# Softmax-normalisation transfers on GpSimd's queue, more staging for w_in, and multiplications of zeros in planned gaps

## The chip, the cores and the metric

The kernel runs on one core of a Trainium2 chip. TensorE (PE) multiplies matrices into PSUM, ScalarE (ACT) computes activations, VectorE (DVE) does elementwise work, SyncE (SP) and GpSimd (POOL) can start DMA transfers, and 16 DMA engines move the bytes. The metric is the device time of one execution in microseconds (us). Before the change the median of 3 runs was 631.99 us (631.64 to 633.69).

## The reference

Attention with a tanh cap on the scores, then a two-layer feed-forward part:

```
scores = cap * tanh(q @ k.T / sqrt(64) / cap)          # 4 batches, 12 heads, 448 tokens, head size 64
attn   = exp(scores - max);  attn /= sum(attn) + 1e-9
x      = (attn @ v), heads side by side                # 1792 x 768
h      = x @ w_in                                      # 768 x 2048
g      = h * sigmoid(1.702 * h)
out    = g @ w_out                                     # 2048 x 768
```

w_in and w_out reach the device as 64-bit floating-point words, which the kernel decodes itself into pairs of float16 (a high and a low part).

## The kernel before

The work is cut into 24 units, one per batch and pair of heads. A unit computes the transposed scores in four groups of key columns: matmuls into the PSUM tile s, tanh on ACT (t<-s), exp on ACT (p<-t), and then, on PE, the sums of the exponentials (tile sm) and the unnormalised output (tile pa). Units 0 to 7 multiply in float32; from unit 8 on everything is split into float16 pairs, which takes more work on ACT and DVE. When a batch's six units are done, its x feeds the first layer (tile m, weights wi_h and wi_l) and then the second (tile m, weights in wo).

The normalisation of a unit (function attend, lines 674 to 707) takes a small detour, because the reciprocal is cheap only if the 896 sums of a unit lie across many partitions: s4 (tile f) is evicted from sm, then a DMA writes it to the DRAM tile sd, a DMA reads it back as 112 partitions x 8 (rsum), DVE takes the reciprocal (rr), a DMA writes it to the DRAM tile rd, and two DMAs read that back, repeated over the partitions (rb). DVE multiplies rb by the unit's output, and ACT or DVE splits the product into xh and xl. Two units of batch 0 (4 and 5) do without this detour (normalise_direct). For units 0 to 7 the output is first evicted from pa to pu, of which there are two buffers; pa is a single PSUM bank. So pa of unit n+1 can begin once unit n is in pu, and that needs the product of unit n-2.

w_in is loaded in 15 pieces of 64-bit words into a staging area in the later storage of w_out (early_w, three pieces of 1024 words per partition) and decoded by five steps per piece: a shift and two bit operations on DVE, a scaling on ACT or DVE, and the split into wi_h and wi_l.

The order of the work is made by a planner (class Plan). It lists all operations with their dependences, gives each a cost (the tables at lines 34 to 44), lets a forward pass choose for each engine what starts first, a backward pass compute due times, and repeats this 20 times (PASSES). The best order is then emitted, and each engine and each DMA queue runs its instructions strictly in that order. All transfers of the kernel before stand in one queue, SP's (function dma, line 199). The planner chooses between ACT and DVE for the operations that both can do (function scaled).

Of the code around the change: fetch_w (line 491) requests a piece, decode_w (line 510) decodes it, h_unit (line 709) makes one 128-column block of the first layer and writes g, and 16 small matmuls of zeros at the very start (lines 393 and 394) run before the first data arrive.

## Time and profile before

| | |
|---|---|
| median of 3 runs | 631.99 us |
| the profiled execution | 636.09 us, of which 633.9 us from the first to the last instruction |
| busy: PE, DVE, ACT | 618.0, 386.3, 393.0 us |
| mean granted share of PE's clock | 0.993 |
| HBM read and written | 54.93 and 5.66 MB |
| transfers in SP's queue | 36,288 packets, 60.61 MB |

In the profile, an instruction is named by its line, its engine, and the tiles it writes and reads, out<-in, with buffer numbers left out. Line 196 holds all planned matmuls, line 202 all planned DMA issues, lines 153, 161, 177 and 184 the ACT and DVE operations, so the tile names tell what an instruction does. A matmul in float32 makes two records per instruction. "wo" as the source of matmuls or of decoding is the area in which q, k, v and w_in are staged early on. SPq is SP's instruction queue. PE's busy time counts a matmul that runs at half clock as busy.

### The profile page before, as it was taken

How to read it: one execution, taken by the hardware profiler on the slowest of the kernel's cores; microseconds unless marked ns; L12 is line 12 of the kernel's file. 1: busy time of each engine (PE TensorE's matmuls, PEld its weight loads, DVE VectorE, ACT ScalarE, POOL GpSimd, SP SyncE). 2: the span in 40 equal slices, each digit the busy share in tenths (PEclk: the TensorE clock that was granted, in tenths of full speed). 3: DMA queues.
4: the chain of work that ended last, by engine and by line, in shares of the span. 5: the costliest groups of instructions: out<-in, count | busy, mean ns of one | idle time of the engine just before them, and what ended most of it. 6: DMA issues, size and time to landing. Idle time of an engine off the chain costs nothing.

```text
span 633.9 us, 9374 instructions
## 1 busy us (share of the span) xinstructions
PE 618.0 (97%) x3666; PEld 292.3 (46%) x3666; DVE 386.3 (61%) x684; ACT 393.0 (62%) x536; POOL 0.2 (0%) x4
## 2 busy tenths in 40 slices
PE   7987999999999999999999999999999999999995
PEld 3322344454444445445445545445445555555552
DVE  5687988999789866696773466696754113331000
ACT  6997897699798777787666467778647113331000
POOL 0000000000000000000000000000000000000000
PEclk9997999999999999999999999999999999999999
DMA  8968651442466732202322312200111100000000
GB/s 303 412 202 206 224 183 49 149 147 82 130 187 197 226 98 64 77 14 76 91 68 80 95 49 82 76 16 19 22 41 45 30 30 1 1 0 17 29 15 34
DMA packets 36339, 61.28 MB, mean 97 GB/s; under 512 B 13928, under 2 KB 21952, under 8 KB 36288
## 3 DMA queue, kind: packets, MB, share of 16 engines
q1 hardware_dynamic: 36288, 60.61, 30.8%
q8 instruction: 30, 0.49, 0.3%
q14 instruction: 21, 0.17, 0.1%
HBM read 54.93 MB, written 5.66 MB: 96 GB/s over the span
## 4 chain that ended last, share of the span: by engine, by line
PE 93%; DMA 4%; DVE 1%; SPq 1%; ACT 0%; issue 0%; DVEq 0%
PE m L196 70%; PE s L196 10%; PE pa L196 10%; PE sm L196 4%; DMA wo<-in_moe_w_in_dram 1%; DMA sd<-f 1%; DMA rb<-rd 1%; DMA wo<-in_v_dram 1%; DMA wo<-in_q_dram 1%; SPq L202 0%; DVE wi_l L161 0%; DVE wo L161 0%; ACT wi_h L177 0%; DVE rb L161 0%; DVE wo L184 0%
## 5 line engine op out<-in xcount | busy, mean ns | idle before, releaser
L196 PE MATMUL m<-gh,wo 128*128 128x448 f16 x768 | 216.2, 353 | 0.0
L196 PEld LDWEIGHTS <-wo 128*128 128x128 f16 x1152 | 110.8, 98 | 107.9 <-issue 7.0
L196 PE MATMUL m<-xh,wi_h 128*128 128x448 f16 x384 | 135.6, 353 | 0.0
L196 PE MATMUL m<-xl,wi_h 128*128 128x448 f16 x384 | 135.3, 352 | 0.0
L196 PE MATMUL m<-gl,wo 128*128 128x448 f16 x384 | 135.3, 352 | 0.0
L196 PE MATMUL m<-xh,wi_l 128*128 128x448 f16 x384 | 135.3, 352 | 0.0
L153 ACT ACTIVATE t<-s,tsc 128x896 f32<-128x896 f32 x96 | 87.1, 908 | 49.1 <-PE s L196 48.9
L196 PEld LDWEIGHTS <-wi_h 128*128 128x128 f16 x768 | 72.8, 98 | 78.7 <-issue 13.7
L161 DVE SCALAR_TENSOR_TENSOR f<-f,m 128x448 f32<-128x448 f32 x64 | 39.5, 618 | 53.1 <-ACT f L153 52.9
L153 ACT ACTIVATE f<-m 128x448 f32<-128x448 f32 x64 | 34.6, 541 | 58.9 <-PE m L196 57.8
L177 ACT ACTIVATE f<-m 128x448 f32<-128x448 f32 x23 | 12.4, 539 | 83.9 <-PE m L196 75.8
L161 DVE TENSOR_TENSOR ta<-ta,t 128x896 f32<-128x896 f32 (+1 forms) x48 | 41.0, 855 | 32.1 <-ACT t L153 30.8
L153 ACT ACTIVATE t<-t,lnb,capt 128x896 f32<-128x896 f32 (+1 forms) x52 | 52.9, 1018 | 1.4
L161 DVE SCALAR_TENSOR_TENSOR wo<-wo 128x1024 int32<-128x1024 int32 (+3 forms) x50 | 51.8, 1051 | 3.2 <-ACT wo L177 2.6
L196 PEld LDWEIGHTS <-wi_l 128*128 128x128 f16 x384 | 37.6, 98 | 35.1
L161 DVE SCALAR_TENSOR_TENSOR gl<-f,gh 128x448 f16<-128x448 f32 x64 | 39.5, 622 | 16.9 <-ACT gh L177 16.3
L161 DVE TENSOR_TENSOR p<-t,p 128x896 f16<-128x896 f32 (+1 forms) x52 | 48.9, 942 | 1.2 <-ACT p L177 0.9
L196 PE MATMUL s<-qh,kk 128*128 128x448 f16 (+3 forms) x160 | 47.5, 401 | 0.0
L177 ACT ACTIVATE p<-t 128x896 f16<-128x896 f32 (+1 forms) x52 | 43.4, 835 | 1.5
L196 PE MATMUL s<-ql,kk 128*128 128x448 f16 (+1 forms) x128 | 39.5, 352 | 0.0
L177 ACT ACTIVATE gh<-f 128x448 f16<-128x448 f32 x51 | 29.1, 571 | 13.8 <-DVE f L161 13.8
L196 PE MATMUL pa<-p,vh 128*64 128x448 f16 x256 | 35.4, 357 | 0.0
(92 smaller groups left out, 539.0 us busy)
## 6 DMA issues: line engine op xcount, KB each, us to landing
wo<-in_moe_w_in_dram SPq DMA_DIRECT2D x24, 512.0 KB
stg<-in_kx_dram SPq DMA_DIRECT2D x16, 448.0 KB
stg<-in_qx_dram SPq DMA_DIRECT2D x16, 448.0 KB
stg<-in_moe_w_out_dram SPq DMA_DIRECT2D x16, 384.0 KB
wo<-in_moe_w_out_dram SPq DMA_DIRECT2D x16, 384.0 KB
out_dram<-f SPq DMA_DIRECT2D x24, 224.0 KB
rb<-rd SPq DMA_DIRECT2D x44, 112.0 KB
vd<-in_v_dram SPq DMA_DIRECT2D x18, 256.0 KB
```

Of the source, the lines that this page charges most:

```text
L153: self.nc.scalar.activation(real(out), real(in_), func, scale=real(scale), **b)
L161: getattr(self.nc.vector, name)(out=real(out), **{k: real(x) for k, x in ins.items()}, **kw, **a)
L177: self.nc.scalar.activation(real(out), real(in_), AF.Copy, scale=1.0 if f is None else f, **b)
L196: self.nc.tensor.matmul(real(o), real(w), real(x), start=a, stop=z)
```

## The change

Four things are changed together.

1. The five small transfers of attend (sd, rsum, rd and the two of rb) go to GpSimd's queue. The planner gets that queue as an engine of its own, with 1.0 us for an issue and a lag of 3.0 us, where SP's has 0.5 and 2.6.
2. The first four pieces of w_in (the first 512 columns) are staged in the storage of g, which is now one tile; it has room for three pieces. The three places of early_w go to the pieces behind them. All four are requested when the first is decoded (G_AHEAD). Writes of g in batch 0 come after the decoding of these pieces.
3. Where the planner's times leave PE idle by more than 0.5 us before the first use of tile m, matmuls of a 128 x 128 tile of zeros are emitted (keep_busy), one for each 0.06 us.
4. The planner's order changes everywhere as a consequence.

```diff
+G_PIECES = 4
+G_AHEAD = 4
+IDLE_MIN, IDLE_STEP = 0.5, 0.06
-LAG = {"PE": 0.23, "ACT": 0.0, "DVE": 0.0, "SP": 2.6}
-DMA_ISSUE, DMA_BW = 0.5, 0.36
+LAG = {"PE": 0.23, "ACT": 0.0, "DVE": 0.0, "SP": 2.6, "POOL": 3.0}
+DMA_ISSUE, DMA_BW = {"SP": 0.5, "POOL": 1.0}, 0.36
+QUEUES = ("SP", "POOL")
+SMALL = "POOL"
...
-    def dma(self, pairs, mb):
+    def dma(self, pairs, mb, queue="SP"):
+        issuer = {"SP": self.nc.sync, "POOL": self.nc.gpsimd}[queue]
         def emit():
             for o, i in pairs:
-                self.nc.sync.dma_start(real(o), real(i))
-        self.op({"SP": (DMA_ISSUE * len(pairs), emit)}, [p[0] for p in pairs], [p[1] for p in pairs], mb=mb)
+                issuer.dma_start(real(o), real(i))
+        self.op({queue: (DMA_ISSUE[queue] * len(pairs), emit)}, [p[0] for p in pairs], [p[1] for p in pairs], mb=mb)
...
     def emit(self):
         with self.tc.manual_schedule():
+            end = None
             for o in self.order:
+                if o.eng == "PE":
+                    if self.idle_bank is not None:
+                        if any(b.ring is self.idle_bank for b in o.bufs):
+                            self.idle_bank = None
+                        elif end is not None:
+                            self.keep_busy(o.turn, o.start - end)
+                    end = o.end
                 o.emit()
+
+    def keep_busy(self, turn, gap):
+
+        rows, cols = (128, 128) if turn == "full" else (int(x) for x in turn.split("x"))
+        z, out = self.zeros, self.idle_bank["tiles"][0]
+        for _ in range(int((gap - IDLE_MIN) / IDLE_STEP)):
+            self.nc.tensor.matmul(out[:cols, :128], z[:rows, :cols], z[:rows], start=True, stop=True)
...
+    plan.zeros, plan.idle_bank = wz, ps_m
...
-    gt = [sb.tile([P, NFC, S], F16, name=nm) for nm in ("gh", "gl")]
-    gs = [tuple(plan.fixed(t[:, fc]) for t in gt) for fc in range(NFC)]
+    g_s = sb.tile([P, 2 * NFC * S], F16, name="g")
+    gs = [tuple(plan.fixed(g_s[:, (i * NFC + fc) * S:(i * NFC + fc + 1) * S]) for i in range(2)) for fc in range(NFC)]
+
+    early_g = plan.ring([words(g_s[:, i * NW:(i + 1) * NW]) for i in range(2 * NFC * S // NW)])
...
-                st = plan.turn(early_w)
-                early_bufs["w"].append(st.buf)
+                at = "g" if z < G_PIECES else "w"
+                st = plan.turn({"g": early_g, "w": early_w}[at])
+                early_bufs[at].append(st.buf)
...
-        for y in range(z, z + W_AHEAD[m + (c > 0 and m)]):
+        for y in range(z, z + (G_AHEAD if z + 1 < G_PIECES else W_AHEAD[m + (c > 0 and m)])):
...
-        plan.dma([(sd, s4[::32])], 0.02)
+        plan.dma([(sd, s4[::32])], 0.02, SMALL)
...
-        plan.dma([(rs, sd.rearrange("(j g) (p m) -> (g p) j m", g=2, m=RW))], 0.02)
+        plan.dma([(rs, sd.rearrange("(j g) (p m) -> (g p) j m", g=2, m=RW))], 0.02, SMALL)
...
-        plan.dma([(rd.rearrange("j (p m) -> p j m", m=RW), rr)], 0.02)
+        plan.dma([(rd.rearrange("j (p m) -> p j m", m=RW), rr)], 0.02, SMALL)
...
-        plan.dma([(rb[j * D:(j + 1) * D], rd[j:j + 1].to_broadcast([D, S])) for j in range(2)], 0.3)
+        plan.dma([(rb[j * D:(j + 1) * D], rd[j:j + 1].to_broadcast([D, S])) for j in range(2)], 0.3, SMALL)
...
+        plan.after = early_bufs["g"] if b == 0 else []
         plan.scaled(gh, t, GS)
         plan.stt(gl, t, GS, gh, ALU.mult, ALU.subtract, accum_out=fcol())
+        plan.after = []
```

How the order changes is shown at three places. The first is SP's queue while units 1 and 2 are computed. Names carry buffer numbers here; wo_119 is the staging area, and sd, rsum belong to the normalisations of units 0 and 1. Before:

```order
L202 DMA wo_119<-in_moe_w_in_dram 128x1024 x4
L202 DMA sd0_151<-f0_139 4x224
L202 DMA wo_119<-in_v_dram 128x512
L202 DMA wo_119<-in_k_dram 128x448
L202 DMA wo_119<-in_q_dram 128x448
L202 DMA wo_119<-in_moe_w_in_dram 128x1024 x2
L202 DMA sd1_152<-f1_140 4x224
L202 DMA wo_119<-in_v_dram 128x512
L202 DMA wo_119<-in_k_dram 128x448
L202 DMA wo_119<-in_q_dram 128x448
L202 DMA rsum_115<-sd0_151 112x2x4
L202 DMA wo_119<-in_moe_w_in_dram 128x1024 x2
```

Now SP's queue at the same stage:

```order
L209 DMA wo_119<-in_q_dram 128x448
L209 DMA wo_119<-in_moe_w_in_dram 128x1024 x4
L209 DMA wo_119<-in_v_dram 128x512 x2
L209 DMA wo_119<-in_k_dram 128x448
L209 DMA wo_119<-in_q_dram 128x448
L209 DMA kk0_125<-in_k_dram 128x448
L209 DMA qh0_127<-in_q_dram 128x448
L209 DMA kk1_126<-in_k_dram 128x448
L209 DMA g_171<-in_moe_w_in_dram 128x1024 x2
L209 DMA qh1_128<-in_q_dram 128x448
```

No small transfer stands in it. They are in GpSimd's queue, here from its first transfer on:

```order
L209 DMA sd0_151<-f0_139 4x224
L209 DMA rsum_115<-sd0_151 112x2x4
L209 DMA rd0_153<-rr0_149 112x2x4
L209 DMA sd1_152<-f1_140 4x224
L209 DMA rb0_142<-rd0_153 64x448 x2
L209 DMA rsum_115<-sd1_152 112x2x4
L209 DMA sd0_151<-f2_141 4x224
L209 DMA rd1_154<-rr1_150 112x2x4
L209 DMA rsum_115<-sd0_151 112x2x4
L209 DMA rb1_143<-rd1_154 64x448 x2
```

So they no longer stand between the loads of w_in, q, k and v, but in one line among themselves: the transfer rd of unit 0, which needs rr, stands in front of sd of unit 1.

The second place is DVE's queue around the first reciprocal of a normalisation (rr0), which reads rsum of unit 0. Before, 36 planned DVE instructions stood ahead of it, 27 of them decoding w_in, six on w_out and three evictions:

```order
L161 SCALAR_TENSOR_TENSOR wo_119<-wo_119 128x1024
L161 TENSOR_SCALAR wo_119<-wo_119 128x1024
L161 SCALAR_TENSOR_TENSOR wo_119<-wo_119 128x1024
L161 RECIPROCAL rr0_149<-rsum_115 112x8
L161 SCALAR_TENSOR_TENSOR wi_l_118<-wo_119,wi_h_117 128x2x512
L184 TENSOR_SCALAR wo_119<-wo_119 128x1024
```

Now:

```order
L167 SCALAR_TENSOR_TENSOR wo_119<-wo_119 128x1024
L190 TENSOR_SCALAR wi_h_117<-wo_119 128x2x512
L167 RECIPROCAL rr0_149<-rsum_115 112x8
L190 TENSOR_SCALAR wo_119<-wo_119 128x1024
L167 TENSOR_SCALAR wo_119<-wo_119 128x1024
L186 TENSOR_SCALAR f1_140<-sm0_157 128x224
```

There are 22 ahead of it now, all of them decoding w_in. The product of unit 0 (rb0<-pu0,rb0) stood ten rows behind this reciprocal and now stands 13 rows behind it.

The third place is PE's queue where unit 3's output begins (pa0<-p2); before it stood behind the scores and a part of the sums of unit 4:

```order
L196 MATMUL s0_155<-wo_119 128x448 x2
L196 MATMUL sm0_157<-p1_135,ones32_2_75 64x448 x2
L196 MATMUL s1_156<-wo_119 64x448 x2
L196 MATMUL s0_155<-wo_119 128x448 x2
L196 MATMUL pa0_158<-p2_136,wo_119 64x448 x2
L196 MATMUL pa0_158<-p3_137,wo_119 64x448 x2
L196 MATMUL pa0_158<-p4_138,wo_119 64x448 x2
L196 MATMUL pa0_158<-p0_134,wo_119 64x448 x2
```

Now:

```order
L349 LDWEIGHTS wz_89
L349 MATMUL m0_91<-wz_89 32x128
L202 MATMUL sm0_157<-p2_136,ones32_2_75 32x224 x4
L202 MATMUL sm0_157<-p3_137,ones32_2_75 32x224 x4
L202 MATMUL pa0_158<-p2_136,wo_119 64x448 x2
L202 MATMUL pa0_158<-p3_137,wo_119 64x448 x2
L202 MATMUL s0_155<-wo_119 128x448 x2
L202 MATMUL s1_156<-wo_119 128x448 x2
```

Unit 3's output now follows the sums of its own exponentials at once. L349 is the last of three matmuls of zeros at this place, of 14 in all; two stand behind the second row of scores of unit 0, and nine before the first scores of unit 2. The first layer's first matmuls stand behind 57 rows of attention matmuls now, before behind 59. Over the whole program PE changes between kinds of matmul 223 times, with those of zeros, before 210 times.

## Rows read from the trace of the kernel before

**Rows 1.** The busy time of each engine in five stretches of the span (us), with the granted share of PE's clock, the share of the 16 DMA engines and GB/s as the last three columns.

```profile
7.00:20.00 13.00, 13.00 (x77) 3.71 (x74) 10.40 (x18) 12.00 (x13) 0.00 (x0) 1.00 1.03 388
20.00:37.20 17.20, 17.20 (x128) 5.55 (x126) 10.74 (x16) 16.17 (x21) 0.00 (x0) 1.00 0.88 349
37.20:59.90 22.70, 16.47 (x87) 4.89 (x87) 19.06 (x23) 20.01 (x24) 0.00 (x0) 0.85 0.82 205
60.00:100.00 40.00, 40.00 (x217) 14.34 (x215) 36.20 (x46) 34.41 (x45) 0.00 (x0) 1.00 0.52 177
...
220.00:630.00 410.00, 407.54 (x2355) 204.22 (x2353) 202.37 (x353) 210.33 (x288) 0.00 (x0) 1.00 0.16 47
```

**Rows 2.** What PE waited for over the whole span: total us, times, longest.

```profile
PE s L196 <- ACT t L153: 3.8, 4, 1.5
PE pa L196 <- ACT pu L177: 2.4, 1, 2.4
```

**Rows 3.** PE's instructions in groups by form, first of the stretch from 0 to 37.2 us, then (from the line with x64) of the stretch from 0 to 59.8 us; the number behind the x counts the records.

```profile
L196 PE MATMUL s<-wo 64*128 64x448 f32 x48 | 14.1, 684 | 1.4 <-DMA wo<-in_q_dram 1.4
L196 PE MATMUL pa<-p,wo 128*64 128x448 f32 x48 | 11.2, 567 | 0.0
L196 PE MATMUL sm<-p,ones 128*32 128x224 f32 x96 | 5.8, 359 | 0.0
L196 PE MATMUL s<-wo 64*64 64x448 f32 x14 | 3.5, 565 | 0.0
...
L196 PE MATMUL s<-wo 64*128 64x448 f32 x64 | 18.1, 660 | 4.1 <-ACT t L153 2.7 <-DMA wo<-in_q_dram 1.4
L196 PE MATMUL pa<-p,wo 128*64 128x448 f32 x64 | 17.3, 662 | 2.4 <-ACT pu L177 2.4
L196 PE MATMUL sm<-p,ones 128*32 128x224 f32 x128 | 7.9, 359 | 0.0
L196 PE MATMUL s<-wo 64*64 64x448 f32 x20 | 4.8, 562 | 1.0 <-ACT t L153 1.0
L196 PE MATMUL sm<-p,ones 128*64 128x448 f32 x8 | 1.9, 552 | 0.0
```

**Rows 4.** From the chain of work that ended last, in order of time (start, us, what, xcount of records), the pieces that give PE's pace, and its first matmuls; the last two lines lie behind 100 us.

```profile
5.17 4.85 PE s L196 x12
12.93 0.90 PE pa L196 x4
13.83 0.95 PE s L196 x4
16.64 0.94 PE sm L196 x16
100.32 16.00 PE m L196 x84
118.11 1.24 PE m L196 x6
```

**Rows 5.** From the instructions in order of time (start, us, engine, line, operation, tiles), the normalisation of unit 0 from the eviction of its sums to the product, and what followed: the eviction of unit 2's output to pu, and unit 3's output.

```profile
17.60 0.39 DVE L180 TENSOR_SCALAR f<-sm 128x224 f32<-128x224 f32 x1 [1.18 <-PE sm L196]
...
22.68 0.64 SPq L202 DMA_DIRECT2D sd<-f  x1
...
31.96 0.42 SPq L202 DMA_DIRECT2D rsum<-sd  x1
...
40.83 0.20 DVE L161 RECIPROCAL rr<-rsum 112x8 f32<-112x8 f32 x1
...
41.05 0.33 SPq L202 DMA_DIRECT2D rd<-rr  x1
...
45.54 1.15 SPq L202 DMA_DIRECT2D rb<-rd  x2
...
51.07 0.63 DVE L161 TENSOR_TENSOR rb<-pu,rb 128x448 f32<-128x448 f32 x1 [1.16 <-DMA rb<-rd]
...
51.73 0.54 ACT L177 ACTIVATE pu<-pa 128x448 f32<-128x448 f32 x1 [1.33 <-DVE rb L161]
...
52.33 6.13 PE L196 MATMUL pa<-p,wo 128*64 128x448 f32 x16 [2.43 <-ACT pu L177]
```

**Rows 6.** The normalisation of the last unit, from the eviction of its sums to the product, when the DMA engines had little else to do.

```profile
495.57 0.36 ACT L177 ACTIVATE f<-sm 128x224 f32<-128x224 f32 x1 [2.73 <-PE sm L196]
...
503.19 2.45 SPq L202 DMA_DIRECT2D rb<-rd  x2
507.97 0.62 DVE L161 TENSOR_TENSOR rb<-pa,rb 128x448 f32<-128x448 f32 x1 [8.35 <-DMA rb<-rd]
```

**Rows 7.** Groups of ACT's and DVE's instructions between 7 and 60 us by form: what one decoding step takes (busy us, mean ns).

```profile
L177 ACT ACTIVATE wi_h<-wo 128x1024 f16<-128x1024 f32 x5 | 5.9, 1171 | 0.4 <-DVE wo L161 0.4
L177 ACT ACTIVATE wo<-wo 128x1024 f32<-128x1024 f32 x4 | 4.6, 1156 | 0.1
L177 ACT ACTIVATE stg<-stg 128x384 f32<-128x384 f32 x2 | 1.1, 544 | 0.0
...
L161 DVE SCALAR_TENSOR_TENSOR wo<-wo 128x1024 int32<-128x1024 int32 x13 | 15.8, 1226 | 1.9 <-ACT wo L177 1.8
L161 DVE TENSOR_SCALAR wo<-wo 128x1024 int32<-128x1024 int32 x7 | 4.8, 691 | 1.5 <-DMA wo<-in_moe_w_in_dram 1.5
```

**Rows 8.** The 16 matmuls of zeros at the start.

```profile
1.91 1.86 PE L394 MATMUL m<-wz,ones 128*32 128x128 f16 x16 [1.91 <-DVE thr L840]
```

More of the change, by code (lines that the diff above doesn't have):

```diff
@@ L222, in forward @@
         self.start_over()
-        free = {"PE": 0.0, "ACT": ACT_FROM, "DVE": ACT_FROM, "SP": 0.0}
+        free = {"PE": 0.0, "ACT": ACT_FROM, "DVE": ACT_FROM, "SP": 0.0, "POOL": 0.0}
         cand = {e: [o for o in self.ops if e in o.ways and not o.left] for e in free}
-        turn, pipe = None, 0.0
+        turn, pipe = None, dict.fromkeys(QUEUES, 0.0)
         order = []
@@ L255, in forward @@
                 done += LAG["PE"]
-            elif e == "SP":
-                pipe = max(pipe, t + us) + o.mb / DMA_BW
-                done = pipe + LAG[e]
+            elif e in QUEUES:
+                pipe[e] = max(pipe[e], t + us) + o.mb / DMA_BW
+                done = pipe[e] + LAG[e]
             order.append(o)
@@ L261, in forward @@
                 u.left -= 1
-                u.ready = max(u.ready, t + us if u.eng == e and e != "SP" else done + HANDOFF)
+                u.ready = max(u.ready, t + us if u.eng == e and e not in QUEUES else done + HANDOFF)
                 if not u.left:
@@ L274, in backward @@
     def backward(self, order):
-        after = {o: [(u, 0.0 if u.eng == o.eng != "SP" else LAG[o.eng] + HANDOFF) for u in o.users] for o in order}
+        after = {o: [(u, 0.0 if u.eng == o.eng and o.eng not in QUEUES else LAG[o.eng] + HANDOFF) for u in o.users] for o in order}
         turns = {}
@@ L295, in backward @@
         due = {o: end for o in order}
-        free = dict.fromkeys(("PE", "ACT", "DVE", "SP"), end)
+        free = dict.fromkeys(("PE", "ACT", "DVE", *QUEUES), end)
         cand = [o for o in order if not left[o]]
@@ L325, in emit @@
         with self.tc.manual_schedule():
+            end = None
             for o in self.order:
-                o.emit()
+                if o.eng == "PE":
+                    if self.idle_bank is not None:
+                        if any(b.ring is self.idle_bank for b in o.bufs):
+                            self.idle_bank = None
+                        elif end is not None:
+                            self.keep_busy(o.turn, o.start - end)
+                    end = o.end
+                o.emit()
+    def keep_busy(self, turn, gap):
[3 more added lines that the diff above has]
+            self.nc.tensor.matmul(out[:cols, :128], z[:rows, :cols], z[:rows], start=True, stop=True)
 def tile_kernel(tc, q, k, qx, kx, v, cap, w_in, w_out, out):
@@ L453, in fast_path @@
     early_v = plan.ring([t.bitcast(F32).rearrange("p (c d) -> p c d", d=D) for t in room(HALF + 6 * NA, NV, 4)])
-    early_bufs = {"w": [], "a": [], "h": []}
+    early_bufs = {"w": [], "a": [], "h": [], "g": []}
     stg_t = [sb.tile([P, 2 * S], F32, name=f"stg{i}") for i in range(4)]
```

## The prediction

> **What bounds the kernel now.** I read the stretches first. PE is busy without a break at full clock from 60 us to the end of its work: 40.00 of 40.00 us, then 407.54 of the 410 us behind 220, and the missing 2.5 are the tail [rows 1]. A PE that is full there can't be helped by better transfers, so a gain must come from the first 60 us. ACT and DVE don't bound the rest either (202 and 210 of 410 us behind 220), though between 60 and 100 us they are busy for 34.4 and 36.2 of 40 us.
>
> Busy time hides gaps inside matmuls, so I count what PE needed. At its pace of 0.95 us for four records of scores, 0.90 for four of pa, 0.94 for sixteen of sm, and 16.00 / 84 = 0.19 for one of the first layer [rows 4], the 60 + 48 + 96 records up to 37.2 us (two of the 62 scores records belong behind it) are 14.25 + 10.8 + 5.64 = 30.7 us [rows 3]. PE began at 5.17 [rows 4], so it had 32.0 and lost 1.3, at the start where nothing is ready. From there to 59.9 us come 24 records of scores, 16 of pa, 32 of sm, 8 of the wide sm [rows 3] and the first three of the first layer: 5.7 + 3.6 + 1.9 + 1.8 + 0.6 = 13.6 us, and PE had 22.7. It lost 9.1 us there. This is the ceiling for the whole change.
>
> The waits say where [rows 2]: 3.8 us for tanh on ACT (t), 2.4 us for pu. With 16.47 us busy of 22.70 [rows 1], 6.2 us are idle. The sixteen pa records behind the pu wait took 6.13 us [rows 5] where the pace gives 3.6: the granted clock fell to its lower level (1.2 of 2.4 GHz) after these idle times; the stretch shows 0.85 on average [rows 1]. That is 2.5 us more; 0.4 stay unnamed.
>
> Both waits have a history. ACT is busy for 16.2 of 17.2 us before 37.2 us and for 20.0 of 22.7 behind it [rows 1], since it decodes w_in beside tanh and exp. And pu waited for unit 0's normalisation, which took from 17.99 to 51.07 us, 33.1 us [rows 5]: sd was issued 4.7 us after the sums were there, because SP stood at loads of w_in that had no place yet; rsum 9.3 later, rr 8.9 after that.
>
> **The change part by part.** *Transfers on GpSimd's queue.* The waits behind SP's loads go (order, first place). The new deadline: unit 3's output now needs pu after 16 rows of scores, 12 of pa, 7 groups of sm and 14 matmuls of zeros: 15.2 + 10.8 + 6.6 + 0.8 = 33.4 us of PE work, so at 5.17 + 1.3 + 33.4 = 39.9 us. Before it come the eviction (0.54) and the product (0.63) [rows 5], so rb must land by 38.7. Unit 0's sums are complete after 6, 3 and 2 such groups, 5.7 + 2.7 + 1.9 = 10.3 us of PE, and evicted in 0.39: at 17.2. The detour may take 21.5 us. No row shows a transfer from GpSimd. The nearest below is the last unit's detour on SP with idle DMA engines, from 495.93 to 507.97 = 12.0 us [rows 6]; the nearest above is unit 0's, 33.1. What load does to a transfer with no queue ahead: rb took 5.5 us from its issue to the product that waited for it at 45.54 [rows 5], against 4.8 at 503.19 [rows 6], so about 0.7 more. Four such steps give 12.0 + 2.8 = 14.8; for GpSimd's own part and for its queue I add 3 and take 18, nearer to the lower row, because queue order made most of the 33. Then pu is in time and the 2.4 + 2.5 us of pu wait and clock go.
>
> *The staging of w_in.* Six places instead of three let DVE decode early: it was busy for only 10.40 + 10.74 of the 30.2 us before 37.2 [rows 1]. This takes work from ACT: up to the last exponential of unit 4, ACT decoded in four steps on wo, five on wi_h and two on stg, now three, two and one of half size. That is 4 x 1.16 + 1.1 - 0.6 = 5.1 us less [rows 7], against three more evictions (0.36 + 2 x 0.54, [rows 5, 6]) 1.4 us: ACT is there 3.7 us earlier. PE's waits for tanh (3.8) shrink; I take half, 1.9 us, as left, because ACT is still only a step or so ahead of PE. The earlier w_in loads push k, q and v back by up to three pieces of 0.52 MB, 4 us at 388 GB/s [rows 1]; k and q of unit 1 are used only some 8 us after unit 0's begin, so I cost this at nothing; without that cover it would be PE idling 1 to 2 us near 13.
>
> *Zeros.* 14 matmuls of 128 columns are 0.054 us each at the first layer's pace (0.19 x 128 / 448), at most 0.116 by the start's 1.86 us for 16 [rows 8]. Two lie in the start's wait; the other twelve cost 0.7 us (1.4 at most) if PE is not idle there, and nothing if it is. They can't give back more than the clock's 2.5 us, which are counted above.
>
> *Changes between kinds of matmul.* 13 more in the program; one costs 1.24 - 6 x 0.19 = 0.1 us [rows 4], so 1.3 us, or nothing where PE waits.
>
> Sum: 9.1 - 1.9 - 0.7 - 1.3 = 5.2 us gained. The profiled execution took 636.09 us, 4.1 more than the median; the part before 60 us is the same in kind, so I subtract from both: 630.9 and 631.99 - 5.2 = 626.8 us.
>
> A rule that speaks against it: rows 7 show DVE's TENSOR_SCALAR steps at 0.69 us for 1024 words, where the two-input steps take 1.23; nine of the fast ones stand in the new order from eight rows ahead of rr0 to the product. The Trainium skill ("SBUF — State Buffer", section "SBUF: two separate sides") says that a transfer started from GpSimd can't write its descriptors while DVE runs in such a two-port mode, and gives 620 ns alone against about 3100 ns beside a copy. If each of five transfers waits for one whole step of 0.69 us, the detour is 18 + 3.5 = 21.5 us, exactly the deadline, and the sum stands without margin. With the page's figure, an estimate of 5 x 2.5 = 12.4 us more, it would be 30 us and the gain gone. No row here shows either.
>
> **The rivals.** *A: ACT and DVE pay it back.* If PE is 5.2 us ahead at 60 us, DVE's 36.2 us of work up to 100 us [rows 1] must fit into 34.8; unless the early decoding takes it forward, DVE is 1.4 us late, and if ACT's 3.8 us of waits stay whole, 1.9 us more are lost: 5.2 - 3.3 = 1.9, so 630.1. For it: both engines are near 90% there. Against: DVE's idle 9 us before 37.2.
>
> *B: the detour is in time only in part.* Between 21.5 and 26.7 us the gain is eaten one for one, because ACT stands at pu and PE behind it; the middle, 24, gives 629.3; at 26.7 it is 632.0.
>
> *C: slower.* Place: rr0 in DVE's queue, 13 rows ahead of the product, with decoding behind it, and pu0 in ACT's. If the small transfers still take the 33.1 us of before, because their bytes wait for the same 16 engines, at 1.03 of their time [rows 1], and GpSimd's queue blocks itself (rd0 stands ahead of sd1), pu is 33.1 - 21.5 = 11.6 us late and the clock falls again for 2.5: 626.8 + 11.6 + 2.5 - 1.9 (waits for tanh that lie inside) = 639.0. It decides from 26.7 us on. The skill's page "DMA: Bandwidth & Descriptors" (section "Issuing engines are not separate DMA queues") says that another issuing engine saves only the issue time; by that rule alone C would be nearer, but the 4.7 and 9.3 us of rows 5 were issue time in SP's line.
>
> *D: nothing moves,* since pu was not what held PE: 632. Against it, rows 2 and 5.
>
> **Chances.** Forecast 0.52 (own range 623.5 to 629.9), A 0.18, B 0.14, C 0.11, D 0.05. A measurement can tell about 0.3% (1.9 us). Faster, below 630.1: 0.52 + 0.12 of A + 0.09 of B = 0.73. Slower, above 633.9: C and little more, 0.11. The same: 0.16. The range runs from 623.0, the ceiling of 9.1 us, to 633.0; above it lies most of C, 0.1.
>
> **What would show it.** Right: between 37 and 60 us PE's busy share near full at clock 1.00, first matmul of the first layer near 50 us instead of 59; unit 0's product before 39.3 us; sd issued within 2 us of its sums; ACT's pu without a wait. Wrong: DVE idle before rr for a transfer, PE waiting for pu, a clock below 1 before 60 us (B, C); PE waiting for t or for decoded weights between 60 and 100 us (A). The price of GpSimd's transfers is the weakest number: a detour above 26.7 us makes the whole forecast wrong.

## The result, and the profile after

| | time, median (lowest to highest) | profiled execution | its span |
|---|---|---|---|
| the kernel before, 10 executions beside the changed one | 634.11 us (631.64 to 636.83) | 636.09 us | 633.9 us |
| the changed kernel, 10 executions | 639.11 us (637.76 to 642.35) | 638.25 us | 636.4 us |

The ratio is 1.0081, with a 95% interval of 1.0063 to 1.0099: slower by 0.6 to 1.0%, some 5 us, where 5.2 us of gain were forecast. In further sets of 10 to 29 executions the kernel before took 633.7 to 634.7 us; the three executions shown ahead of the prediction were at the low end.

The stretches of [rows 1], for the changed kernel:

```profile
7.00:20.00 13.00, 13.00 (x78) 3.85 (x76) 11.39 (x17) 12.17 (x16) 0.73 (x1) 1.00 1.03 404
20.00:37.20 17.20, 16.92 (x133) 6.15 (x133) 14.06 (x17) 15.54 (x21) 4.03 (x6) 1.00 1.02 381
37.20:59.90 22.70, 19.16 (x109) 6.22 (x107) 18.12 (x28) 17.82 (x23) 6.05 (x10) 0.92 0.60 183
60.00:100.00 40.00, 40.00 (x230) 14.84 (x227) 36.65 (x45) 36.65 (x48) 3.01 (x5) 1.00 0.47 170
...
220.00:630.00 410.00, 404.70 (x2336) 201.89 (x2334) 198.14 (x345) 210.47 (x289) 38.26 (x63) 1.00 0.14 44
```

Up to 100 us this reads like a gain: PE is busy for 19.16 us instead of 16.47 between 37.2 and 59.9 us, at a mean granted clock of 0.92 instead of 0.85. The share of the DMA engines between 20 and 37.2 us has gone up from 0.88 to 1.02. And in the last line PE is busy for 2.84 us less than before, because it is done earlier. The chain of waits dates that: the last two matmuls of the program, which in the kernel before are

```profile
627.39 0.17 PE sm L196 x2
```

are in the changed kernel

```profile
624.55 0.17 PE sm L202 x2
```

So in these two executions PE ended 2.84 us earlier, and the program 2.5 us later. What lies behind PE's end is not counted as busy and stands in no group of the page. It is seen when one asks for the last line of the program, where the engines meet. First the kernel before, then the changed one (q: the engine's sequencer; duration in ns, least, median and most; first and last start in us):

```profile
L1028 POOLq DRAIN  x3: 34/41/78, 629.0 to 633.7; - x3
L1028 SPq DRAIN  x3: 7/7/13, 633.1 to 633.5; - x3
```

```profile
L1056 POOLq DRAIN  x3: 44/102/9119, 626.5 to 636.2; - x3
L1056 SPq DRAIN  x3: 7/7/7, 630.6 to 635.9; - x3
```

GpSimd closes its part of a program with a DRAIN. Before, it took 0.04 us and began at 629.0, 4.1 us before the other engines came to the meeting at 633.1. Now it begins at 626.5 and takes 9.12 us, until 635.6. The others are there at 630.6 and wait 5.0 us.

The waits of PE [rows 2] are now, without the two of the program's start:

```profile
PE pa L202 <- ACT pu L183: 3.5, 1, 3.5
...
PE sm L202 <- DVE f L186: 0.3, 1, 0.3
```

The waits for tanh (3.8 us) are gone; the wait for pu has grown from 2.4 to 3.5. Unit 0's normalisation [rows 5] now lies on the chain of waits from end to end (start, us, what):

```profile
17.46 0.37 ACT f L183
...
18.12 4.62 DMA sd<-f
...
23.04 4.95 DMA rsum<-sd
...
28.02 0.21 DVE rr L167
...
28.51 6.03 DMA rd<-rr
...
35.36 6.51 DMA rb<-rd
...
41.97 0.64 DVE rb L167
...
42.69 0.55 ACT pu L183
...
43.29 2.68 PE pa L202 x8
```

From the sums (17.8) to the product (41.97) it is 24.2 us instead of 33.1, and four landings make up 22.1 of them. Nobody stands in a line any more; the transfers themselves are slow. How slow, compared with the rest of the program, is shown by the landings of the transfers that write or read rd (rd and rb together), and then by those of rb alone, first between 15 and 60 us:

```profile
DMA to landing us min/median/max: 2.5/5.9/6.5
```

```profile
DMA to landing us min/median/max: 2.8/6.0/6.5
```

and then, in the same order, between 220 and 510 us, where the DMA engines are busy for 0.14 of the time:

```profile
DMA to landing us min/median/max: 1.9/2.7/4.5
```

```profile
DMA to landing us min/median/max: 2.6/2.8/4.5
```

The last unit's detour shows the price of GpSimd's queue without load [rows 6]. First on SP, in the kernel before, then on GpSimd:

```profile
495.95 0.52 SPq L202 DMA_DIRECT2D sd<-f  x1
...
497.57 0.33 SPq L202 DMA_DIRECT2D rsum<-sd  x1
...
499.21 0.20 DVE L161 RECIPROCAL rr<-rsum 112x8 f32<-112x8 f32 x1 [5.03 <-DMA rsum<-sd]
...
500.87 0.34 SPq L202 DMA_DIRECT2D out_dram<-f  x1
501.31 0.38 SPq L202 DMA_DIRECT2D rd<-rr  x1
```

```profile
493.94 0.61 POOL L209 DMA_DIRECT2D sd<-f  x1 [11.98 <-ACT f L183]
495.87 0.68 POOL L209 DMA_DIRECT2D rsum<-sd  x1 [1.32 <-DMA sd<-f]
...
498.12 0.20 DVE L167 RECIPROCAL rr<-rsum 112x8 f32<-112x8 f32 x1 [6.27 <-DMA rsum<-sd]
...
498.61 0.67 POOL L209 DMA_DIRECT2D rd<-rr  x1 [2.06 <-DVE rmin L876]
501.19 1.07 POOL L209 DMA_DIRECT2D rb<-rd  x2 [1.91 <-DMA rd<-rr]
504.74 0.62 DVE L167 TENSOR_TENSOR rb<-pa,rb 128x448 f32<-128x448 f32 x1 [6.22 <-DMA rb<-rd]
```

From its sums at 493.65 it is 11.1 us, on SP it was 12.0. The single small transfer is not quicker on GpSimd: from sd to rsum, from rsum to rr and from rd to rb it takes 1.93, 2.25 and 2.58 us, where SP took 1.62, 1.64 and 1.88, so 0.3 to 0.7 us more each. What GpSimd saves is the line: on SP, rd was issued 1.9 us after rr, behind a transfer of the output, and the two transfers of rb took 2.45 us to issue, where GpSimd took 1.07.

### The profile page after: what moved, and what is told of

It is laid out like the page before. It is cut to its first block, busy times and chain, and to the rows that moved or that the text cites. A ratio compares the mean times of both kernels' runs of the same rounds, so it can differ in the third digit from the quotient of the medians.

```text
span 636.4 us, 9410 instructions
## 1 busy us (share of the span) xinstructions
PE 617.6 (97%) x3680; PEld 292.5 (46%) x3680; DVE 384.4 (60%) x678; ACT 394.4 (62%) x542; POOL 67.7 (11%) x114
## 3 DMA queue, kind: packets, MB, share of 16 engines
q0 software_dynamic: 4224, 5.29, 3.4%
## 4 chain that ended last, share of the span: by engine, by line
PE 93%; DMA 4%; issue 0%; DVE 0%; ACT 0%; SPq 0%; POOL 0%; DVEq 0%; ACTq 0%
PE m L202 69%; PE s L202 11%; PE pa L202 9%; PE sm L202 4%; DMA rb<-rd 1%; DMA rd<-rr 1%; DMA rsum<-sd 1%; DMA sd<-f 1%; DMA wo<-in_q_dram 1%; DVE rb L167 0%; ACT pu L183 0%; POOL rb L209 0%; SPq L209 0%; SPq L397 0%; ACT f L183 0%
## 5 line engine op out<-in xcount | busy, mean ns | idle before, releaser
L202 PE MATMUL m<-g,wo 128*128 128x448 f16 x1152 | 226.7, 353 | 0.0
L167 DVE SCALAR_TENSOR_TENSOR g<-f,g 128x448 f16<-128x448 f32 x64 | 39.5, 622 | 17.2 <-ACT g L183 16.8
L167 DVE SCALAR_TENSOR_TENSOR wo<-wo 128x1024 int32<-128x1024 int32 (+2 forms) x42 | 44.5, 1073 | 2.0 <-ACT wo L183 1.7
L183 ACT ACTIVATE g<-f 128x448 f16<-128x448 f32 x52 | 29.8, 573 | 15.7 <-DVE f L167 15.6
L202 PE MATMUL s<-ql,kk 128*128 128x448 f16 (+1 forms) x128 | 39.5, 352 | 0.0
L209 POOL DMA_DIRECT2D sd<-f x22 | 13.8, 626 | 216.7 <-ACT f L183 160.7
```

The source lines that it names most:

```text
L167: getattr(self.nc.vector, name)(out=real(out), **{k: real(x) for k, x in ins.items()}, **kw, **a)
L183: self.nc.scalar.activation(real(out), real(in_), AF.Copy, scale=1.0 if f is None else f, **b)
L202: self.nc.tensor.matmul(real(o), real(w), real(x), start=a, stop=z)
L209: issuer.dma_start(real(o), real(i))
```

## The experiments

The theory after this has two parts: the end of the program costs 5 us that no part of the prediction has, and unit 0's detour is too long by its load, so that the first 60 us gain nothing either. The rivals: the loss is not at the end at all; the detour is slow because it is on GpSimd; the zeros, the staging or the planner's new order do the harm. No kernel leaves out a part of the computation. Ratios are to the kernel before, in sets of executions of their own, and need not be the quotient of two medians; where that matters, both are given.

| run | what it is | time, us | ratio, 95% interval |
|---|---|---|---|
| before_again | the kernel before | 634.81 | 1.0004 (0.9986 to 1.0023) |
| one_on_gpsimd | before, one transfer on GpSimd | 634.77 | 1.0006 (0.9984 to 1.0029) |
| early_drain | changed, DRAIN also behind the last transfer | 635.25 | 1.0016 (1.0001 to 1.0030) |
| no_zeros | early_drain without zeros | 634.93 | 1.0010 (0.9987 to 1.0032) |
| sp_queue | changed, small transfers on SP, 191 zeros | 640.87 | 1.0101 (1.0082 to 1.0120) |
| sp_no_zeros | the same without zeros | 642.03 | 1.0139 (1.0119 to 1.0159) |
| no_staging | early_drain without staging, 2 zeros | 634.18 | 1.0004 (0.9984 to 1.0023) |
| plan_slow_detour | no_zeros, planned with 6 us a landing | 633.79 | 1.0003 (0.9983 to 1.0023) |
| four_units | changed, GpSimd for four units, no zeros | 635.32 | 1.0013 (0.9991 to 1.0036) |
| four_units_no_staging | the same without staging | 628.06 | 0.9917 (0.9892 to 0.9942) |
| four_units_slow_plan | that, planned with 5 us a landing | 630.25 | 0.9940 (0.9919 to 0.9960) |
| swap_all | before's order, GpSimd for all units, early DRAIN | 632.81 | 0.9976 (0.9956 to 0.9997) |
| swap_four | before's order, GpSimd for four units | 633.55 | 0.9999 (0.9980 to 1.0017) |
| best_all_gpsimd | four_units_no_staging's order, GpSimd for all, early DRAIN | 628.71 | 0.9921 (0.9897 to 0.9946) |
| best_again | four_units_no_staging once more | 627.56 | 0.9920 (0.9890 to 0.9950) |
| load_beside | the same and 1.6 MB of loads nobody reads | 631.55 | 0.9955 (0.9936 to 0.9973) |

**The end: does the DRAIN cost a fixed time, or a time for each transfer?** one_on_gpsimd issues one transfer of the kernel before from GpSimd:

```diff
-                self.nc.sync.dma_start(real(o), real(i))
+                (self.nc.gpsimd if pool else self.nc.sync).dma_start(real(o), real(i))
...
-        plan.dma([(sd, s4[::32])], 0.02)
+        plan.dma([(sd, s4[::32])], 0.02, pool=len(rsums) == 12)
```

> The kernel before with a single small transfer (sd of the thirteenth normalised unit, 3.5 KB) issued from GpSimd, everything else in the same order. Theory F: the changed kernel loses at its end because GpSimd's DRAIN, once the engine has issued any transfer, takes a fixed 9.1 us (626.51 to 635.63 in the changed kernel) and the other engines wait for it; then the DRAIN here is 8 to 10 us as well, and as it would start near 629.0 and the others arrive at 633.2, the span is 4.5 to 5.5 us longer than that of the kernel before: about +5 us of time. Theory N (rival): the DRAIN grows with the number of transfers, 9.1 us / 132 issues = 0.07 us each; then it stays near 0.1 us and the time is that of the kernel before within 1 us. Theory C (rival): the loss does not come from the end at all; then no change either, and the DRAIN is short.

early_drain is the changed kernel with the DRAIN called once more, right behind the last small transfer:

```diff
                 o.emit()
+                if o is small[-1]:
+                    behind()
...
-    plan.emit()
+    plan.emit(lambda: nc.gpsimd.drain())
```

> The changed kernel with one more DRAIN on GpSimd directly behind its last transfer, some 120 us before the end, with the order of everything else unchanged. If the 9.1 us are work that is done once and that piles up with the transfers, the early DRAIN takes some 9 us beside PE's work, the last one under 0.5 us, and the end comes 5.0 us earlier: the time falls from about 639 to 634 and stands 0 to 3 us below the kernel before. If every DRAIN behind a GpSimd transfer costs its 9 us anew, the last one still takes about 9 us and the time stays at 639. If the DRAIN waits for something that happens only at the end of the program, the early one is short and the last one long, and the time stays too.

The DRAIN of one_on_gpsimd, then the two of early_drain (L900 is the added one, L1059 the program's end):

```profile
L1028 POOLq DRAIN  x3: 40/89/140, 629.5 to 634.8; - x3
```

```profile
L900 POOLq DRAIN  x1: 9722/9722/9722, 503.9 to 503.9; - x1
```

```profile
L1059 POOLq DRAIN  x3: 38/102/107, 628.5 to 633.2; - x3
```

Theory N holds, and F falls: one transfer makes the DRAIN 0.14 us long instead of 0.04, 110 transfers (not the 132 of the expectation) make it 9.1 to 9.7. It is work that can be done early: behind the last transfer it takes its 9.7 us while PE multiplies, and at the end 0.11 are left. The time falls from 639.11 to 635.25 us, by 3.9. (The trace's 5.0 us belong to one execution.) four_units, below, fills in the middle: 20 transfers, 1.77 us.

```profile
L1057 POOLq DRAIN  x3: 34/102/1770, 629.1 to 633.8; - x3
```

That is 0.083 to 0.10 us for each transfer. (1, 20 and 110 transfers are 32, 768 and 4224 packets in the traces, so the runs do not tell whether the DRAIN goes by transfers or by what they consist of.) GpSimd has 4.1 us to spare at the end of the kernel before, so by an estimate some 49 transfers would go unseen here (4.1 / 0.083); 110 do not.

With 635.25 us the changed kernel without its end is still not faster than the one before: 1.0016, interval 1.0001 to 1.0030, where 0 to 3 us of gain were expected of it. The 5.2 us of gain are missing as well.

**The parts alone.** sp_queue, sp_no_zeros, no_zeros and no_staging change one or two of the numbers at the head of the changed kernel; the last two have the early DRAIN:

```diff
-SMALL = "POOL"
+SMALL = "SP"
...
-IDLE_MIN, IDLE_STEP = 0.5, 0.06
+IDLE_MIN, IDLE_STEP = 1e9, 0.06
...
-G_PIECES = 4
-G_AHEAD = 4
+G_PIECES = 0
+G_AHEAD = 3
```

> The changed kernel with the small transfers back on SP's queue; staging in g's storage and zeros stay; the planner orders anew. Theory F gives a short end again (0.1 us DRAIN): 5.0 us less there. What the detour then does decides the rest. If the queue was what shortened unit 0's detour (33.1 us before, 24.2 us changed), it is 28 us or more again, pu is waited for by PE for more than the 3.5 us of the changed kernel, and PE ends no earlier than in the kernel before: 632 to 637. If the staging shortened it or made up for it, PE ends 2 to 3 us earlier than before: 629 to 632.

> The changed kernel with the small transfers on SP's queue and no zeros (on SP the planner had put in 191 of them, and the time of 640.87 us is therefore not that of the queue alone): staging alone is left. Theory Z: the zeros made that kernel slow: 177 more of them at 0.054 us are 9.6 us of PE work; without them the time falls to 631 to 635 and PE waits for pu or t where they stood. Theory S: SP's queue made it slow (detour of unit 0 40.1 us); then the time stays above 638 and the waits of PE grow by some 8 us, at a lower clock behind them.

Theory S holds: 640.87 us with zeros (of sp_queue 632 to 637 had been expected), 642.03 without. With the staging, still more loads of w_in, q, k and v stand ahead of the small transfers in SP's line: in sp_no_zeros sd of unit 0 is issued 11.0 us after its sums, the detour takes 40.0 us, and PE waits for it. The two lines below are its waits, and its stretch from 37.2 to 59.9 us:

```profile
PE pa L202 <- ACT pu L183: 8.5, 2, 7.4
PE s L202 <- ACT t L159: 4.0, 6, 1.2
```

```profile
37.20:59.90 22.70, 11.20 (x72) 3.30 (x70) 17.88 (x24) 18.83 (x22) 0.00 (x0) 0.86 0.65 209
```

The same stretch of sp_queue, with 191 zeros in the program, holds the clock:

```profile
37.20:59.90 22.70, 20.67 (x235) 12.52 (x233) 18.26 (x24) 19.02 (x23) 0.00 (x0) 1.00 0.61 204
```

So zeros in number do keep the granted clock at 1.00, and are worth 1.2 us by the medians (2.4 by the ratios) where PE would wait long; 14 of them did not keep it (0.92 in the changed kernel). So the change's queue is needed once the staging is there: the staging without it, in the order that the planner makes of it, is slower by 1.4%.

> The changed kernel with the early DRAIN and without the 14 matmuls of zeros, all else in the same order. If the zeros lie on PE's path, as the prediction has it, PE reaches the wait for pu 0.7 to 1.4 us earlier and gains nothing there, since it then waits that much longer: the time stays at 635.2 within 0.7. If they are what keeps the clock up before that wait, the granted clock falls earlier or longer without them and the time rises by 1.5 us or more. If they hold up unit 0's sums (two stand ahead of them), the detour starts 0.1 to 0.2 us earlier and the time falls by no more than that.

Without zeros 634.93 us, with them 635.25: within what a set can tell. The wait for pu is 4.6 us instead of 4.9, the clock of 37.2 to 59.9 us 0.92 as with them. The 14 zeros do next to nothing in either direction.

> The changed kernel with the early DRAIN, but no pieces of w_in in g's storage; the planner then finds room for 2 zeros instead of 14. With the early DRAIN the changed kernel took 635.25 us, unit 0's detour 25.5 us at a share of the 16 DMA engines of 1.02 between 20 and 37 us, PE's wait for pu 4.9 us. Theory L: the detour is slow because its transfers share the 16 engines with the w_in pieces that the staging pulls forward. Then the share between 30 and 37 us falls to 0.7 to 0.9 as in the kernel before, the detour takes 16 to 21 us, the wait for pu is under 1 us and the time falls to 631 to 633 (0.7 of waits for tanh may come back). Theory Q (rival): the price is that of a transfer from GpSimd itself; then the detour stays at 23 to 26 us and the time at 634.5 to 637.

Between the two theories: the share of the DMA engines between 30 and 37.2 us is 0.83 instead of 1.04, the detour takes 22.0 us, the wait for pu is 2.0 in two pieces, the clock stays at 1.00, and the first layer's first matmul comes at 44.1 us. But the time is 634.18, where Theory L gave 631 to 633. Another wait has taken over:

```profile
PE pa L202 <- ACT pu L183: 2.0, 2, 1.6
...
PE m L202 <- DVE xl L167: 1.3, 1, 1.3
PE s L202 <- ACT t L159: 1.1, 1, 1.1
PE pa L202 <- DVE rb L167: 0.4, 1, 0.4
```

```profile
60.00:100.00 40.00, 37.06 (x212) 13.39 (x209) 36.63 (x43) 34.82 (x46) 2.92 (x4) 1.00 0.50 175
```

PE now lacks 2.9 us between 60 and 100 us, where it had been full in the kernel before. That looked like rival A, and the next runs were to tell.

**The planner's price, and GpSimd for a few units.** plan_slow_detour tells the planner what a landing takes under load; four_units uses GpSimd where the detour matters only, and has no early DRAIN; the last two of this group leave out the staging as well:

```diff
-LAG = {"PE": 0.23, "ACT": 0.0, "DVE": 0.0, "SP": 2.6, "POOL": 3.0}
+LAG = {"PE": 0.23, "ACT": 0.0, "DVE": 0.0, "SP": 2.6, "POOL": 6.0}
...
+        small = SMALL if len(rsums) < 4 else "SP"
-        plan.dma([(sd, s4[::32])], 0.02, SMALL)
+        plan.dma([(sd, s4[::32])], 0.02, small)
```

> The changed kernel with the early DRAIN, no zeros, and a planner that is told that a transfer from GpSimd lands 6.0 us after its issue instead of 3.0 (the trace shows 4.6 to 7.8 us per step for unit 0). It moves unit 3's output behind more rows of scores and sums. If the wait for pu is the loss that is left, it goes (under 1 us) with the stretch at the lower clock, and the time falls by 3 to 5 us against 635.25, to 630 to 632. If ACT's decoding holds PE anyway (rival A of the prediction), waits for t or for decoded weights take its place and the time is 633 to 636.

> The changed kernel with GpSimd's queue for the first four normalised units only (20 transfers), SP's for the other 18, no zeros, no early DRAIN. If the DRAIN goes by the number of transfers, it takes 20 x 0.083 to 20 x 0.10 = 1.7 to 2.0 us and ends before the other engines arrive (GpSimd has about 4 us to spare in the kernel before), so nothing of it is seen in the time: 633 to 636, as with the early DRAIN (635.25, without zeros 634.93). If the DRAIN's length had a fixed part that only shows above some number, it would be known by a length outside 1.5 to 2.2 us.

> As four_units, without the staging in g's storage. The kernel without staging reached the first layer at 44.1 us instead of 55.5 and kept the clock, but then waited for xl, tanh and pu between 60 and 100 us. If that loss comes from the later units' detours on GpSimd (unit 6 took 69.5 us), SP's queue for them takes it away and the time is 631 to 633. If it comes from ACT and DVE, which are busy for 35 to 37 of these 40 us, as rival A says, the waits stay and the time is 633.5 to 635.5.

> As four_units_no_staging, with a planner that takes 5.0 us instead of 3.0 for the landing of a GpSimd transfer. If the waits for pu that were left (1.6 us the longest) are what still costs, they go and the time falls 1 to 2 us below that of four_units_no_staging. If ACT and DVE set the pace up to 100 us, the waits only move and the two are the same within 1 us.

plan_slow_detour shrinks the wait for pu to 1.2 us, but waits for tanh (2.5) and for p (2.4) come in its place: 633.79 us, in the range expected by rival A (633 to 636), and a gain of nothing beside the kernel before. four_units is early_drain again, with the tail covered. And four_units_no_staging takes 628.06 us, below both ranges expected of it: a gain of 5.3 us by the ratio of 0.9917 and of 6.6 by the medians. So a gain of the size that the prediction had put at 5.2 us is there, with one part of the change (the queue, for four units), without the other two, and in an order of its own. Its planner's slower twin takes 630.25, with a wait of 2.1 us for rb: the expected gain of 1 to 2 us was a loss of 2.

**With the order held still.** Until here every run had an order of its own, since the planner starts anew with each number. In swap_all and swap_four the planner still sees SP's queue, and the transfers are issued from GpSimd when the order is written out; in best_all_gpsimd likewise with four_units_no_staging's order. PE, ACT, DVE and the bulk loads on SP then have the very order of the kernel they come from.

```diff
-                self.nc.sync.dma_start(real(o), real(i))
+                (self.nc.gpsimd if pool else self.nc.sync).dma_start(real(o), real(i))
```

> The kernel before in its own order on PE, ACT, DVE and SP, with all 110 small transfers issued from GpSimd instead of SP, and the early DRAIN. PE's order is laid out there for a product of unit 0 at 51 us, so an earlier one can take away at most the wait for pu (2.5 us) and the stretch at the lower clock behind it (1.7 to 3.4 us), the waits for tanh (3.7) stay. If the queue alone shortens the detour from 33 us to 24 or less, the wait for pu goes and the time falls by 2.5 to 5 us against the kernel before, to 629.5 to 632. If the detour stays at 30 or more because rr and the product stand where they stood in DVE's queue, the time is that of the kernel before within 1 us.

> As swap_all, but only the 20 small transfers of the first four normalised units from GpSimd, no early DRAIN (it should take 1.77 us and be covered). If the later units' queue does not matter, the same time as swap_all within 0.7 us; if the later units' transfers on GpSimd cost something (each lands a little later behind the bulk loads, unit 6 above all), swap_four is faster than swap_all by 1 us or more.

The detour stays at 32.1 and 31.8 us, since rr stands where it stood in DVE's queue (rsum is issued at 25.4 us, lands within 4.8 to 6.9 us, and rr starts at 39.95). The wait for pu falls from 2.5 us to 1.5 and 1.1. 632.81 and 633.55 us: the queue without the order that goes with it is worth 0.2 to 0.9 us by the medians, and by swap_all's interval 2.8 at most.

> The kernel four_units_no_staging in its own order, with all 110 small transfers from GpSimd and the early DRAIN. If the later units' queue is what made no_staging 6.1 us slower, the time is 632 or more here, with waits for xl, pu or t between 60 and 220 us. If it was the order that the planner made, the time stays at 628 to 629.5.

> The kernel four_units_no_staging, unchanged, run again. If its 628.06 us hold, 627.3 to 629.2 and a ratio to the kernel before of 0.988 to 0.994.

best_again: 627.56 us, so the gain holds. best_all_gpsimd: 628.71, so the later units' queue costs about 1 us and not 6. It has the same queue and early DRAIN as no_staging (634.18) and no staging either; what differs are the planner's order and 2 zeros. So 5.5 us by the medians (5.3 by the ratios) between two kernels made of the same parts, but for the 2 zeros, come from the order. Which of its differences does it stays open.

```diff
+            first = [o for o in self.order if o.eng == "POOL"][4]
...
+                if o is first:
+                    beside()
...
+        for t in early_g["tiles"][:3]:
+            nc.sync.dma_start(t[:, :512], w_in.bitcast(I32)[:P, :1024].rearrange("p (w t) -> p w t", t=2))
```

> The kernel four_units_no_staging in its own order, with three more loads of 0.52 MB of w_in into storage of g that nobody reads, issued on SP near 31 us, where SP otherwise waits until 39.7 us: 1.6 MB or 3.9 us of the 16 engines at 400 GB/s, as the staging has them busy there (share 1.04 between 30 and 37 us, where four_units_no_staging shows 0.83). Theory L: unit 0's detour, 21.0 us without them, takes 23 to 25 us, PE waits for pu or xl for 1.5 to 4 us, and the time rises from 628 to 630 to 633. Rival: the plan alone made the staged kernels slow; then the detour stays at 21 to 22 us and the time within 1 us of 628.

The last run tests what load does to the detour. First what PE waited for in best_again, behind the start, two stretches, and unit 0's product, then those of load_beside, which differs by three loads on SP alone. In both, unit 0's sums are evicted by 16.5 us.

```profile
PE s L202 <- ACT t L159: 1.4, 2, 0.8
```

```profile
20.00:37.20 17.20, 17.20 (x117) 5.54 (x116) 11.64 (x21) 15.26 (x19) 5.19 (x8) 1.00 0.95 364
37.20:59.90 22.70, 21.92 (x126) 6.68 (x124) 21.42 (x28) 22.57 (x27) 7.65 (x12) 1.00 0.62 179
```

```profile
37.88 0.63 DVE L167 TENSOR_TENSOR rb<-pu,rb 128x448 f32<-128x448 f32 x1 [0.24 <-DMA rb<-rd]
```

```profile
PE s L202 <- ACT t L159: 2.6, 3, 1.1
...
PE pa L202 <- ACT pu L183: 1.2, 1, 1.2
PE m L202 <- DVE xl L167: 0.7, 1, 0.7
```

```profile
20.00:37.20 17.20, 17.20 (x117) 5.54 (x116) 12.08 (x21) 14.85 (x18) 4.57 (x8) 1.00 1.03 402
37.20:59.90 22.70, 19.18 (x111) 5.70 (x108) 18.45 (x24) 19.30 (x24) 6.81 (x10) 1.00 0.65 206
```

```profile
41.66 0.63 DVE L167 TENSOR_TENSOR rb<-pu,rb 128x448 f32<-128x448 f32 x1 [3.61 <-DMA rb<-rd]
```

The share between 20 and 37.2 us goes from 0.95 to 1.03, unit 0's detour from 21.4 to 25.1 us, PE loses 2.7 us of work before 59.9 us, and the time is 631.55 us: 3.5 to 4.0 more by the medians, 2.2 to 2.4 by the ratios. No execution of load_beside (631.0 to 632.1) is as fast as one of the other two (627.5 to 629.1). Theory L holds: 1.6 MB of loads beside the detour, as the staging brings them, cost 2 to 4 us by themselves.

> The kernel before, unchanged, to have the span and granted clock of each of its executions beside those of the others. The profiled execution shown before took 636.09 us with a stretch of 6.8 us at the lower clock; if that stretch is there in every execution, the clocks of all runs are alike and the time is 632 to 636; if it comes and goes, mean clock and time vary together, by up to 2.5 us.

before_again: mean clock and time do vary together. Of the 29 executions of the kernel before beside it, the eight at a mean clock of 0.997 or more took 631.4 to 633.3 us, the others, at 0.992 to 0.995, 633.3 to 636.6: a spread of 5 us, where 2.5 had been expected. Its profiled execution has 0.92 between 37.2 and 59.9 us where the one ahead of the prediction had 0.85 [rows 1].

## Why the prediction was wrong, point by point

**The step that failed first: the sum ended with PE.** "PE is busy without a break ... and the missing 2.5 are the tail": I took the tail as given. The change put 110 transfers on an engine that had had none, and that engine's last act is a DRAIN of 0.083 us for each. By the trace this is 5.0 us, by early_drain 3.9 us of the 5.0 that the kernel lost. The trace of before shows the DRAIN at 0.04 us and the 4.1 us that cover it; it could not show the price, but a bound from above was due there.

**The second: "I add 3 and take 18".** The detour took 24.2 us. Of the terms, the lower row held (12.0 us; 11.1 on GpSimd), and what I added as 3 for GpSimd's own part and its queue is about -1 in sum: three small transfers that each land 0.3 to 0.7 us later, against the line that they no longer stand in. The load is not 4 x 0.7 = 2.8 but 24.2 - 11.1 = 13. I had read the 0.7 from one transfer (rb of [rows 5], issued at 45.54 us, where the share from 45 to 52 us was 0.85), while unit 0's transfers now run between 18 and 42 us, where the share is 0.98 to 1.04 and a landing takes 4.6 to 6.5 us. Most of these 13 us are not the staging's: without it, and in other orders, unit 0's detour on GpSimd still takes 21.0 to 22.0 us (four_units_no_staging, best_again, best_all_gpsimd, no_staging), beside bulk loads that the kernel before has too (share 0.95 between 20 and 37.2 us). So 18 was 3 to 4 us short even then, and the staging brought 2 to 4.5 us more (24.2 to 25.5 us in the changed order).

**The third: "so I cost this at nothing".** I looked for the price of the earlier w_in loads in k and q of unit 1, near 13 us. It fell on the detour: load_beside shows 3.8 us of detour and 2.2 to 4.0 us of time for 1.6 MB, in one and the same order. Every staged kernel that uses GpSimd's queue (633.79 to 635.32, the end taken away) is slower than four_units_no_staging and its twin (628.06, 630.25); no_staging, at 634.18, is not better than they are, and there the order is to blame. How much of the staged kernels' loss is load and how much order is therefore settled only as far as load_beside goes.

**What was right.** The deadline: the detour may take 21.5 us. In the changed order 24.2, 25.2 and 25.5 us gave waits for pu of 3.5, 4.6 and 4.9: the detour less the wait is 20.6 to 20.7 us each time, so from there on it is one for one. At 21.4, in another order, there is no wait. The waits for tanh fell from 3.8 us to nothing, where I had left 1.9; that the staging did it, as the prediction says, is not shown: two kernels without it wait 1.1 us for tanh (no_staging, four_units_no_staging), and one with it 4.0 (sp_no_zeros). The zeros: 0.7 us forecast, 0.3 measured and within the noise. The size of the gain: 5.2 us forecast for a detour in time, 5.3 to 6.6 us measured in four_units_no_staging; since the order alone is worth as much between two other kernels, that this agrees so well is partly luck. The thirteen more changes between kinds of matmul (1.3 us) were not measured by themselves.

**The rivals.** The prediction's own signs of being wrong came: DVE idle for 1.94 us before rr, PE waiting for pu, a clock of 0.92 before 60 us. B happened up to PE's end: a detour of 24.2 us for B's 24, and PE 2.8 us earlier for B's 2.7, in the profiled pair. But by an estimate 1.6 us of that pair are the clock of the one execution of before (22.7 us at 0.85, against 0.92 in before_again); over many executions nothing of it is left (early_drain, 1.0016). From the forecast gain of 5.2 go the 2.4 of the wait for pu and the 2.5 of the clock, since both are still there, and 1.0 to 2.4 us for the longer wait; 1.9 more came from tanh. That is between 1.2 us gained and 0.2 lost; with early_drain's own wait of 4.9 us it is 0.2 lost, where its interval shows 0.1 to 1.9: up to 1.7 us that no run here names. C gave 639.0 us, the time measured, by a mechanism of which only a part occurred. The transfers did wait beside the bulk loads; but rd of unit 0 did not hold up sd of unit 1 (issued 0.3 us after its sums), the detour was 24.2 us and not 33.1, the wait for pu 3.5 us and not 11.6, and what made up the time lay at the end. A right number by luck, and "from 26.7 us on" was never reached. A is not seen in the changed kernel (40.00 of 40.00 us between 60 and 100). It is what no_staging looks like, but best_all_gpsimd keeps PE busy for 39.5 of these 40 us with the same work on ACT and DVE, so those two engines did not force it.

**The rules of the Trainium skill.** The transfers' issue on GpSimd took 0.52 to 1.03 us in all 110 cases of the changed kernel, the 1.03 once, beside DVE's fast steps; in the other runs the longest was 1.61 us, once, in plan_slow_detour. So the delay that the Trainium skill ("SBUF — State Buffer", section "SBUF: two separate sides") describes cost at most 0.4 us in the changed kernel and at most 1.0 anywhere, and not the 2.5 us each that the prediction estimated from its figures. The Trainium skill ("DMA: Bandwidth & Descriptors", section "Issuing engines are not separate DMA queues") says that another issuing engine saves only the issue time. The landings of 4.6 to 6.5 us beside bulk loads that came from SP agree with it; what the queue saved was the 4.7 and 9.3 us in SP's line [rows 5], and the load stayed.

## What to carry to other kernels

Follow a change to the last instruction of the program, on every engine it touches, not only on the one that bounds it: an engine that issues transfers for the first time brings its own end. A small transfer with a deadline is priced under the load that lies beside it, and under what the same change adds; here the part that was to feed the decoders early slowed the part that was to be quick. And where a planner orders everything anew, run each part in a frozen order too: the same parts differed by some 5 us with the order.

## What the runs showed of the hardware that was not expected

GpSimd's DRAIN takes 0.14 us behind 1 transfer, 1.77 behind 20, 9.1 to 9.7 behind 110, though all of them had landed 120 us before; done early, it is not due again. Without load a small transfer takes 0.3 to 0.7 us longer on GpSimd's queue than on SP's (1.93, 2.25, 2.58 against 1.62, 1.64, 1.88 us), yet the four steps are done sooner (11.1 against 12.0 us), since nothing stands ahead of them. A 3.5 KB transfer lands in 2.1 to 2.7 us (medians) when the DMA engines have little to do, and unit 0's three took 4.6 to 6.0 when they were full, though the bulk came from another queue. And one and the same kernel varies by 5 us from execution to execution (631.4 to 636.6), along with its mean granted clock (0.998 to 0.992).
